# Layer A's small matmuls in groups of 32 columns

## The chip, the cores and the metric

One core of a Trainium2 chip. The core has a matrix engine (TensorE; its weight loads are shown apart as PEld), VectorE (DVE), ScalarE (ACT), GpSimd (POOL) and SyncE (SP), and 16 DMA engines that move data between the chip's memory and the on-chip buffers. Each engine works through its own queue of instructions in order; semaphores tell one engine that another has finished. The metric is the time of one execution on the device, in microseconds (us): the median of several runs.

## The reference

Four layers, A B A B, over x of 2048 rows by 640. Only layer A matters here: a transformer with a recurrent memory, 32 heads of 192, segments of 32 rows behind 8 memory rows.

```
for s in range(n_seg):                       # 64 segments
    xs = x[:, s*seg_len:(s+1)*seg_len, :]
    h = concatenate([mem, xs], axis=1)       # 8 + 32 rows
    q, k, v = h @ Wq, h @ Wk, h @ Wv         # per head
    scores = (q @ k^T) * scale
    scores = where(mask, scores, -1e9)
    o = softmax(scores) @ v
    o = o @ Wo
    mem = o[:, :M, :]                        # the next segment's memory
    outs.append(o[:, M:, :])
```

The memory ties the segments together: no projection of a segment can be finished before the output of the segment before it is known.

## The kernel before, in words

Each layer A has a preparation (`A_pre`), which computes what does not depend on the memory (keys, queries and values of the last 8 rows of all segments), and the chain (`A_chain`), which runs over the 64 segments one after the other. Layer A runs twice, so there are 128 segments. The order of the chain's instructions on each engine is the order in which the program writes them (`manual_schedule`).

A segment works on its 32 heads in four rounds of eight heads each; even segments run the rounds 0 to 3, odd ones 3 to 0, so that the weights of the turning round stay in place. The rows of `hT` are 8 memory rows and the first 24 of the segment; the last 8 rows come from the preparation's results, loaded as `kqb` and `vb` by GpSimd's DMA queue. Scores are held as 80 keys by 4 times 80 queries: 64 for a pair of heads' 32 rows and 16 for their last 8.

One round is made of these steps:
- Projections (`project`, L988): Q, K and V, each 5 pieces of 128 inputs, each piece 4 matmuls of 32 weight columns (`hT`) by 384 moving columns. The four go to partitions 0, 32, 64 and 96 of the result (`tile_position=(0, 32 * g)`), so that they use the array's four groups of 32 columns. Q and K are copied by ScalarE to `raw` (L998, one buffer) and transposed by VectorE into `QT` (L1006 to L1008) and `KT` (L1003); GpSimd adds the last 8 rows' parts (L964 to L967). V is copied into `Vp` by ScalarE (L1017) and VectorE (L1019).
- `scores`: a mask matmul (L1025, 80 weight columns) and six score matmuls (L1030, 80 weight columns by 80 or 160) into `ps_s`. `weigh` lets ScalarE take the exponential (L1085) into `E`.
- `sums` (L1099): a matmul of ones by `E`, 80 weight columns by 320, back into `ps_s`; ScalarE takes Ln and Exp of it (L1104, L1105) and VectorE multiplies `E` (L1106).
- `attend` (L1038): for each of two halves four matmuls of 128 weight columns (`Vp`) by 80. One 128-row part of the output holds two heads, so that it takes two of the four matmuls, added up. ScalarE and VectorE copy the result to `OT` (L1044, L1045) and the last rows' share to `otb` (L1051 to L1054), which GpSimd's queue stores.
- `wo_round` (L1067): 12 steps of 4 matmuls, 32 weight columns by 160, added up in `ps_w` over all rounds.

The rounds overlap. In round n the TensorE stream is: Q projection of n+1, `attend` of n-1, scores of n, K projection of n+1, `sums` of n, in round 1 also the output round of round 0, V projection of n+1. The first projections of a segment are Q, K and V of round 0 and Q and K of round 1. The segment ends with the last V projection (the second round's output matmuls between its pieces), the last scores, the third `attend`, `sums`, the third output round, the last `attend`, and the last output round. Then VectorE transposes the memory rows out of `ps_w` (L1220, L1221) into the next `hT`.

`keep_busy` (L1074) issues matmuls whose result nobody reads, at the segment's end, before waits; `fill` (L1080) issues weight loads of a single column that nobody uses: 2 in each segment (`SEG_FILL`), and 86 or 79 in a layer's first segment (`FILL`).

Weights: part of them stays in the buffer; 3 of 5 pieces of Q, K and V share slots between two rounds. `load_slot` reloads a slot on SyncE's queue as soon as round 0's projection has read it, and `load_wo` reloads the shared output weights after the first output round (`wo_rows`). SyncE's loads of a segment are 18: Q 3, K 6, V 3, output 6.

Of the kernel before, what the change touches and what calls it, by code (L numbers as in the profile page):

```python
# [17 lines left out]
SLOTS = {"Q": 3, "K": 3, "V": 3}  # L18
LN_EPS = 1e-5

FILL = {0: 86, 2: 79}
SEG_FILL = 2

LATE = 64512
ARENA = 202752
# [2 lines left out]
def ap3(ap, dims):  # L28
    return bass.AP(tensor=ap.tensor, offset=ap.offset, ap=[list(d) for d in dims])
# [86 lines left out]
class Kernel:  # L116
# [799 lines left out]
    def A_chain(self, xn_dram, at_dram, li, load_slot, piece, load_wo, late_wo, wo_mid, wo_end, low):  # L916
        nc, tc, KC, NSEG = self.nc, self.tc, self.KC, self.NSEG
        scale = float(self.Dh) ** -0.5
        NR = 4
        with tc.tile_pool(name=f"A{li}_ch", reuse_waits="tile", bufs=1) as sp, \  # L920
# [3 lines left out]
            KT = sp.tile([P, 6, 80], BF16, name="KT")  # L924
            QT = sp.tile([P, 2, 4, 80], BF16, name="QT")
            Vs = [sp.tile([P, 896], BF16, name=f"Vp{i}") for i in range(2)]
# [11 lines left out]
            def load_rows(s):  # L938
                nc.gpsimd.dma_start(out=xr[8:32, :], in_=xn_dram[32 * s:32 * s + 24, :])
# [61 lines left out]
            def to_rows(raw, m):  # L1001
                if m == "K":
                    nc.vector.transpose(out=KT[:, :, 0:64], in_=raw[:, :].rearrange("p (c j) -> p c j", j=64))  # L1003
                else:
                    rv = raw[:, :].rearrange("p (x i j) -> p x i j", i=3, j=64)
                    nc.vector.transpose(out=QT[:, :, 0:4:3, 0:64], in_=rv[:, :, 0:3:2, :])  # L1006
                    nc.vector.transpose(out=QT[0:64, :, 1, 0:64], in_=rv[0:64, :, 1, :])
                    nc.vector.transpose(out=QT[64:P, :, 2, 0:64], in_=rv[64:P, :, 1, :])  # L1008

            def v_rows(pv, n, which="ax"):  # L1010
                for x in range(2):
# [6 lines left out]
                    else:  # L1018
                        nc.vector.tensor_copy(out=o, in_=i)  # L1019

            def scores():

                S = pop.tile([P, 512], F32, name="ps_s", tag="s", bufs=2)
                m = self.mk[0:80, :]
                nc.tensor.matmul(S[0:80, 0:320], lhsT=self.ident[0:80, 0:80], rhs=ap3(m, [list(m.ap[0]), [0, 4], [1, 80]]),  # L1025
                                 start=True, stop=False, skip_group_check=True)
                for x in range(2):
                    for i, q0, q1 in ((0, 0, 1), (1, 1, 3), (2, 3, 4)):
                        c0 = 160 * x + (80 if i == 2 else 0)
                        nc.tensor.matmul(S[0:80, c0:c0 + 80 * (q1 - q0)], lhsT=KT[:, 3 * x + i, :], rhs=QT[:, x, q0:q1, :],  # L1030
                                         start=False, stop=(x == 1 and i == 2), skip_group_check=True)
                return S

            def attend(E, n, OT=None):
                O = [pop.tile([P, 512], F32, name=f"ps_o{x}", tag=f"o{x}") for x in range(2)]
                for x in range(2):
                    for k, e, i in ((0, 0, 0), (320, 1, 2), (128, 0, 1), (192, 1, 1)):
                        nc.tensor.matmul(O[x][:, 80 * i:80 * i + 80], lhsT=Vs[n % 2][0:80, 448 * x + k:448 * x + k + 128],  # L1038
                                         rhs=E[0:80, 160 * x + 80 * e:160 * x + 80 * e + 80], start=(k == 0),
                                         stop=(k == 192), skip_group_check=True)  # L1040
                if OT is None:
                    OT = sp.tile([P, 6, 64], BF16, name="OT", tag="OT")
                o = [x[:, 0:240].rearrange("p (i q) -> p i q", q=80) for x in O]
                nc.scalar.activation(out=OT[:, 0:3, :], in_=o[0][:, :, 0:64], func=ACT.Copy)  # L1044
                nc.vector.tensor_copy(out=OT[:, 3:6, :], in_=o[1][:, :, 0:64])  # L1045
                return OT, o
# [15 lines left out]
            def wo_round(W, r, OT, first, last, part=range(12)):  # L1062
                w = low[:, 0:7680] if last_wo == r else wo_end[:, :] if r in (0, 3) else wo_mid[:, 7680 * (r - 1):7680 * r]
                for i in part:
                    c, q = i % 6, 32 * (i // 6)
                    for g in range(4):
                        nc.tensor.matmul(W[32 * g:32 * g + 32, 0:160], lhsT=OT[:, c, q:q + 32],  # L1067
                                         rhs=w[:, 640 * i + 160 * g:640 * i + 160 * g + 160], start=(first and i == 0),
                                         stop=(last and i == 11), tile_position=(0, 32 * g), skip_group_check=True)

            def keep_busy(ps, n, w=384):

                for _ in range(n):
                    nc.tensor.matmul(ps[:, 0:w], lhsT=self.ident[:, :], rhs=wo_mid[:, 0:w], start=True, stop=True,  # L1074
                                     skip_group_check=True)

            def fill(n):

                for _ in range(n):
                    nc.tensor.ldweights(self.ident[:, 0:1])  # L1080

            def weigh(last):
                S = scores()
                E = sp.tile([P, 384], BF16, name="E3", tag="raw") if last else sp.tile([P, 320], BF16, name="E", tag="E")
                nc.scalar.activation(out=E[0:80, 0:320], in_=S[0:80, 0:320], func=ACT.Exp, scale=scale)  # L1085
                return S, E
# [9 lines left out]
                        kqs.append(load_kqb(*turns[at + 2]))  # L1096

            def sums(S, E):
                nc.tensor.matmul(S[0:80, 0:320], lhsT=ap3(self.ones_blk[0:80, :], [list(self.ones_blk[0:80, :].ap[0]), [0, 80]]), rhs=E[0:80, 0:320], start=True, stop=True,  # L1099
                                 skip_group_check=True)  # L1100

            def normalise(S, E):
                rc = S[0:80, 0:320]
# [17 lines left out]
            for s in range(NSEG):  # L1121
# [6 lines left out]
                def q_or_k(m, n):  # L1128
                    ps = pqp.tile([P, 512], F32, name="ps_qk", tag="qk")
                    project(hT, ps, m, n, s, range(KC))  # L1130
                    return to_raw(ps, "OT" if m == "K" and n == 0 else "raw")
# [11 lines left out]
                if s == 0:  # L1143
                    fill(FILL[li])
                to_rows(q_or_k("K", 0), "K")
# [10 lines left out]
                for n in range(L):  # L1156
                    raw = q_or_k("Q", n + 1)
                    if n > 0:
                        OT, o = attend(Ep, n - 1)
                        tails_after(n - 1)  # L1160
                    S, E = weigh(False)
                    to_rows(raw, "Q")
                    if n > 0:
                        otb = keep_tail(o)
                    next_kq(s, n)
                    if n > 0:
                        store_tail(otb, s, order[n - 1])
                    to_rows(q_or_k("K", n + 1), "K")
                    sums(S, E)
                    normalise(S, E)  # L1170
                    if n == 1:
                        wo_round(W, order[n - 1], OT, True, False)
                        if n == 1:
                            if s < NSEG - 1:
                                load_wo(order[L])
                            else:
                                tails = [self.fetch_tails(tb, low) for tb in range(2)]
                    if n + 1 < L:
                        pv = v_banks()
                        project(hT, pv, "V", n + 1, s, range(KC))  # L1180
                        v_rows(pv, n + 1)
                    Ep = E
# [5 lines left out]
                v_rows(pv, L)  # L1188
                S, E = weigh(True)
                OT, o = attend(Ep, L - 1, KT[:, :, 0:64])  # L1190
                tails_after(L - 1)
                otb = keep_tail(o, True)
                next_kq(s, L)
                store_tail(otb, s, order[L - 1])
                wo_round(W, order[L - 2], OT1, False, False, range(6, 8))
                sums(S, E)
                wo_round(W, order[L - 2], OT1, False, False, range(8, 12))
                normalise(S, E)
# [2 lines left out]
                    hx_transpose(hT, range(1))  # L1201
                wo_round(W, order[L - 1], OT, False, False)
                idle = pqp.tile([P, 512], F32, name="ps_idle", tag="qk")
                keep_busy(idle, 4, 96)
                OT, o = attend(E, L)
                tails_after(L)
                if s == NSEG - 1:
                    self.first_tails = tails, [self.spread_tails(0, tails[0], low, "vvss")]
                if s + 1 < NSEG:
                    hx_transpose(hT, range(1, 4))  # L1210
                    if s + 2 < NSEG:
                        load_rows(s + 2)
                keep_busy(idle, 5, 230)
                wo_round(W, order[L], OT, False, True)
                keep_busy(idle, 5, 230)
                fill(SEG_FILL)
                if s + 1 < NSEG:
                    wt = sp.tile([P, KC, 32], F32, name="wt", tag="raw")
# [86 lines left out]
```

## Time and profile before

| what | value |
|---|---|
| runs | 3599.22 us median of 3 (3597.11 to 3600.25) |
| the profiled execution: its span | 3590.5 us |
| granted TensorE clock, mean | 0.993 |
| instructions in the span | 168460 |
| DMA | 929.38 MB, mean 259 GB/s |
| one projection quad to the next, 4 x 384 columns | 162 ns |
| one output quad to the next, 4 x 160 columns | 69 ns |
| one `attend` matmul to the next, 128 x 80 | 35 to 36 ns |

The span is that of one execution under the profiler, from its first to its last instruction; a run's time has the launch around it, which makes the 3599.22 us of the median 8.7 us more than the span. In an answer on groups of instructions a line shows the kernel's line, the engine, the operation, what it writes and reads, how often, its busy time, and the idle time of the engine before it with what ended that. In a timeline the first two columns are start and duration in us. Matmuls overlap: their ends are modelled, and a better measure of a stream is the distance from one start to the next.

### The profile page before, as it was taken

How to read it: one execution, taken by the hardware profiler on the slowest of the kernel's cores; microseconds unless marked ns; L12 is line 12 of the kernel's file. 1: busy time of each engine (PE TensorE's matmuls, PEld its weight loads, DVE VectorE, ACT ScalarE, POOL GpSimd, SP SyncE). 2: the span in 40 equal slices, each digit the busy share in tenths (PEclk: the TensorE clock that was granted, in tenths of full speed). 3: DMA queues.
4: the chain of work that ended last, by engine and by line, in shares of the span. 5: the costliest groups of instructions: out<-in, count | busy, mean ns of one | idle time of the engine just before them, and what ended most of it. 6: DMA issues, size and time to landing. Idle time of an engine off the chain costs nothing.

```text
span 3590.5 us, 168460 instructions
## 1 busy us (share of the span) xinstructions
PE 3465.5 (97%) x70978; PEld 2268.6 (63%) x71399; DVE 2327.0 (65%) x6320; ACT 2032.0 (57%) x5233; POOL 1589.1 (44%) x4173
## 2 busy tenths in 40 slices
PE   9989999999999999999999899999999999999999
PEld 7756666666666666655377566666666666666553
DVE  5466666667666666746633566666666666676465
ACT  3356666666566656646432556666666666666463
POOL 3445555555555555530123455555545555555400
PEclk9999999999999999999999999999999999999999
DMA  8988888888788878860476878887888888888600
GB/s 311 334 290 288 281 295 282 278 292 299 278 284 295 289 277 278 295 224 3 146 272 217 290 275 287 290 291 278 285 294 279 290 282 292 292 281 287 222 1 30
DMA packets 452689, 929.38 MB, mean 259 GB/s; under 512 B 75338, under 2 KB 218330, under 8 KB 448858
## 3 DMA queue, kind: packets, MB, share of 16 engines
q1 hardware_dynamic: 382266, 817.56, 64.0%
q0 software_dynamic: 67744, 87.80, 7.9%
q8 instruction: 557, 9.13, 1.0%
q10 hardware_dynamic: 1920, 13.24, 0.9%
q14 instruction: 202, 1.65, 0.1%
HBM read 848.50 MB, written 73.73 MB: 257 GB/s over the span
## 4 chain that ended last, share of the span: by engine, by line
PE 55%; DMA 20%; issue 9%; DVE 7%; POOL 5%; ACT 4%; SPq 1%; PEld 0%; POOLq 0%; ACTq 0%; DVEq 0%
PE ps_qk L988 17%; DMA arena<-wo_rows 7%; DMA Vp<-vb 6%; PE ps_v L988 6%; PE ps_w L1067 6%; PE ps_pre L878 3%; PE ps_o L1038 3%; PE ps_s L1030 3%; DVE hT L943 2%; PE ps_s L1099 2%; DMA arena<-in_A_Wv_dram 2%; PE ps_s L1025 2%; PE ps_pre L902 2%; PE ps_idle L1074 2%; PE kv L1260 1%
## 5 line engine op out<-in xcount | busy, mean ns | idle before, releaser
L988 PEld LDWEIGHTS <-hT 128*32 128x32 bf16 x30720 | 746.5, 96 | 431.9 <-DVE hT L1221 27.2
L988 PE MATMUL ps_qk<-arena,hT 128*32 128x384 bf16 x20480 | 998.8, 328 | 14.6 <-DMA arena<-in_A_Wq_dram 4.2
L998 ACT ACTIVATE raw<-ps_qk 128x384 bf16<-128x384 f32 x1024 | 502.0, 490 | 383.7 <-PE ps_s L1099 250.9
L988 PE MATMUL ps_v<-arena,hT 128*32 128x384 bf16 x10240 | 534.6, 328 | 8.7 <-DMA arena<-in_A_Wv_dram 8.4
L971 POOL DMA_DIRECT2D Vp<-vb x512 | 258.4, 505 | 611.4 <-PE ps_o L1038 465.6
L1067 PE MATMUL ps_w<-arena,OT 128*32 128x160 bf16 x18432 | 446.1, 234 | 11.4 <-DMA arena<-wo_rows 10.4
L1003 DVE STREAM_TRANSPOSE KT<-raw 128x384 bf16<-128x384 bf16 x512 | 296.0, 578 | 194.5 <-ACT raw L998 190.5
L1067 PEld LDWEIGHTS <-OT 128*32 128x32 bf16 x18432 | 322.7, 96 | 103.8 <-ACT OT L1044 22.3
L1006 DVE STREAM_TRANSPOSE QT<-raw 128x256 bf16<-128x256 bf16 x512 | 227.9, 445 | 237.5 <-ACT raw L998 195.5
L959 POOL DMA_DIRECT2D kqb<-kqb x512 | 290.9, 568 | 168.9 <-POOL KT L967 147.3
L1019 DVE CAST Vp<-ps_v 64x384 bf16<-64x384 f32 x512 | 286.2, 559 | 113.6 <-ACT Vp L1017 90.0
L1106 DVE TENSOR_TENSOR E<-E,ps_s 80x320 bf16<-80x320 bf16 x512 | 247.4, 483 | 142.7 <-ACT ps_s L1105 142.3
L1058 POOL DMA_DIRECT2D otb<-otb x512 | 282.7, 552 | 128.1 <-DVE otb L1054 100.0
L1017 ACT ACTIVATE Vp<-ps_v 64x384 bf16<-64x384 f32 x512 | 246.1, 481 | 138.4 <-PE ps_v L988 122.9
L1038 PEld LDWEIGHTS <-Vp 80*128 80x128 bf16 x4096 | 189.9, 99 | 123.1 <-issue 80.5
L1038 PE MATMUL ps_o<-E,Vp 80*128 80x80 bf16 x4096 | 233.0, 201 | 31.8 <-DMA Vp<-vb 15.0
L1085 ACT ACTIVATE E<-ps_s 80x320 bf16<-80x320 f32 x512 | 221.4, 432 | 68.0 <-PE ps_s L1030 33.6
L951 ACT ACTIVATE Vp<-ps_w 32x160 bf16<-32x160 f32 x512 | 150.3, 294 | 155.1 <-DVE wt L1220 138.4
L964 POOL COPY QT<-kqb 128x64 bf16<-128x64 bf16 x512 | 124.5, 243 | 254.8 <-PE ps_s L1030 248.5
L1030 PE MATMUL ps_s<-QT,KT 128*80 128x80 bf16 (+1 forms) x3072 | 233.2, 213 | 1.6 <-POOL KT L967 1.5
L1104 ACT ACTIVATE ps_s<-ps_s 80x320 f32<-80x320 f32 x512 | 214.7, 419 | 31.2 <-PE ps_s L1099 31.2
L1030 PEld LDWEIGHTS <-KT 128*80 128x80 bf16 x3072 | 205.4, 119 | 28.7 <-issue 18.3
(156 smaller groups left out, 5446.4 us busy)
## 6 DMA issues: line engine op xcount, KB each, us to landing
arena<-wo_rows SPq DMA_DIRECT2D x780, 320.0 KB, 6.8
arena<-in_A_Wq_dram SPq DMA_DIRECT2D x427, 384.0 KB, 4.4
arena<-in_A_Wv_dram SPq DMA_DIRECT2D x427, 384.0 KB, 6.6
arena<-in_A_Wk_dram SPq DMA_DIRECT2D x768, 192.0 KB, 4.6
kqb<-kqb POOLq DMA_DIRECT2D x512, 48.0 KB, 5.1
arena<-in_A_Wk_dram SPq DMA_DIRECT2D x43, 384.0 KB, 7.8
vb<-arena POOLq DMA_DIRECT2D x128, 112.0 KB, 6.3
Vp<-vb POOLq DMA_DIRECT2D x512, 28.0 KB, 4.8
```

The source lines that it names most:

```text
L959: nc.gpsimd.dma_start(out=kqb[:], in_=self.kqb_d[r, :, s, :])
L971: nc.gpsimd.dma_start(out=Vs[n % 2][64:80, :], in_=self.vb_d[s, r].rearrange("g t f -> (g t) f"))
L988: nc.tensor.matmul(o[32 * g:32 * g + 32, 0:384], lhsT=hT[:, b, :], rhs=rhs, start=(i == 0), stop=(i == KC - 1), tile_position=(0, 32 * g), ...
L998: nc.scalar.activation(out=raw[:], in_=ps[:, 0:384], func=ACT.Copy)
L1003: nc.vector.transpose(out=KT[:, :, 0:64], in_=raw[:, :].rearrange("p (c j) -> p c j", j=64))
L1017: nc.scalar.activation(out=o, in_=i, func=ACT.Copy)
L1019: nc.vector.tensor_copy(out=o, in_=i)
L1030: nc.tensor.matmul(S[0:80, c0:c0 + 80 * (q1 - q0)], lhsT=KT[:, 3 * x + i, :], rhs=QT[:, x, q0:q1, :], start=False, stop=(x == 1 and i == 2 ...
L1038: nc.tensor.matmul(O[x][:, 80 * i:80 * i + 80], lhsT=Vs[n % 2][0:80, 448 * x + k:448 * x + k + 128], rhs=E[0:80, 160 * x + 80 * e:160 * x ...
L1058: nc.gpsimd.dma_start(out=self.otb_d[:, s, 96 * r:96 * r + 96], in_=otb[:, :, :].rearrange("p c t -> p (c t)"))
L1067: nc.tensor.matmul(W[32 * g:32 * g + 32, 0:160], lhsT=OT[:, c, q:q + 32], rhs=w[:, 640 * i + 160 * g:640 * i + 160 * g + 160], start=(firs ...
L1106: nc.vector.tensor_tensor(out=E[0:80, 0:320], in0=E[0:80, 0:320], in1=rc, op=ALU.mult)
```

## The change

Mask, scores, sums, attention and the filler matmuls are split along their weight columns into matmuls of at most 32 columns, each with a `tile_position` of its own, as the projections and the output round already are. 80 keys become three groups (32, 32, 16). In `attend` each group of 32 output rows belongs to one head, so the part that holds two heads no longer needs two added matmuls: 8 matmuls become 24. Per `scores` 7 matmuls become 21, per `sums` 1 becomes 3. The filler calls get other counts and widths, and each filler becomes four matmuls. Each matmul has its own weight load. The constants of `fill` change too.

```diff
-FILL = {0: 86, 2: 79}
-SEG_FILL = 2
+FILL = {0: 25, 2: 78}
+SEG_FILL = 0
...
+            keys = ((0, 32), (32, 64), (64, 80))
+
             def scores():
...
-                nc.tensor.matmul(S[0:80, 0:320], lhsT=self.ident[0:80, 0:80], rhs=ap3(m, [list(m.ap[0]), [0, 4], [1, 80]]),
-                                 start=True, stop=False, skip_group_check=True)
+                for k0, k1 in keys:
+                    nc.tensor.matmul(S[k0:k1, 0:320], lhsT=self.ident[0:80, k0:k1], rhs=ap3(m, [list(m.ap[0]), [0, 4], [1, 80]]),
+                                     start=True, stop=False, tile_position=(0, k0), skip_group_check=True)
                 for x in range(2):
                     for i, q0, q1 in ((0, 0, 1), (1, 1, 3), (2, 3, 4)):
                         c0 = 160 * x + (80 if i == 2 else 0)
-                        nc.tensor.matmul(S[0:80, c0:c0 + 80 * (q1 - q0)], lhsT=KT[:, 3 * x + i, :], rhs=QT[:, x, q0:q1, :],
-                                         start=False, stop=(x == 1 and i == 2), skip_group_check=True)
+                        for k0, k1 in keys:
+                            nc.tensor.matmul(S[k0:k1, c0:c0 + 80 * (q1 - q0)], lhsT=KT[:, 3 * x + i, k0:k1],
+                                             rhs=QT[:, x, q0:q1, :], start=False, stop=(x == 1 and i == 2),
+                                             tile_position=(0, k0), skip_group_check=True)
...
             def attend(E, n, OT=None):
...
-                    for k, e, i in ((0, 0, 0), (320, 1, 2), (128, 0, 1), (192, 1, 1)):
-                        nc.tensor.matmul(O[x][:, 80 * i:80 * i + 80], lhsT=Vs[n % 2][0:80, 448 * x + k:448 * x + k + 128],
-                                         rhs=E[0:80, 160 * x + 80 * e:160 * x + 80 * e + 80], start=(k == 0),
-                                         stop=(k == 192), skip_group_check=True)
+                    for i in range(3):
+                        for g in range(4):
+                            e = (4 * i + g) // 6
+                            v = 448 * x + 128 * i + 32 * g + 64 * e
+                            nc.tensor.matmul(O[x][32 * g:32 * g + 32, 80 * i:80 * i + 80], lhsT=Vs[n % 2][0:80, v:v + 32],
+                                             rhs=E[0:80, 160 * x + 80 * e:160 * x + 80 * e + 80], start=(i == 0),
+                                             stop=(i == 2), tile_position=(0, 32 * g), skip_group_check=True)
...
             def keep_busy(ps, n, w=384):
...
-                    nc.tensor.matmul(ps[:, 0:w], lhsT=self.ident[:, :], rhs=wo_mid[:, 0:w], start=True, stop=True,
-                                     skip_group_check=True)
+                    for g in range(4):
+                        nc.tensor.matmul(ps[32 * g:32 * g + 32, 0:w], lhsT=self.ident[:, 0:32], rhs=wo_mid[:, 0:w], start=True,
+                                         stop=True, tile_position=(0, 32 * g), skip_group_check=True)
...
             def sums(S, E):
-                nc.tensor.matmul(S[0:80, 0:320], lhsT=ap3(self.ones_blk[0:80, :], [list(self.ones_blk[0:80, :].ap[0]), [0, 80]]), rhs=E[0:80, 0:320], start=True, stop=True,
-                                 skip_group_check=True)
+                ones = self.ones_blk[0:80, :]
+                for k0, k1 in keys:
+                    nc.tensor.matmul(S[k0:k1, 0:320], lhsT=ap3(ones, [list(ones.ap[0]), [0, k1 - k0]]), rhs=E[0:80, 0:320],
+                                     start=True, stop=True, tile_position=(0, k0), skip_group_check=True)
...
-                keep_busy(idle, 4, 96)
+                keep_busy(idle, 1, 256)
                 OT, o = attend(E, L)
...
-                keep_busy(idle, 5, 230)
+                keep_busy(idle, 1, 384)
                 wo_round(W, order[L], OT, False, True)
-                keep_busy(idle, 5, 230)
+                keep_busy(idle, 2, 512)
                 fill(SEG_FILL)
```

## The prediction

> **What bounds the kernel now.** I read the page first, then segments of the two layer A chains: 2 x 64 of them, some 2,690 us of the 3,590.5 us span. From the first projection of a segment (called S) to the next, the trace has 21.14 us in the mean of 124 inner segments (shortest 20.56). TensorE is busy 97% by modelled ends, so its starts matter, and what ends its waits.
>
> ```profile
> PE 3465.5 (97%) x70978; PEld 2268.6 (63%) x71399; DVE 2327.0 (65%) x6320; ACT 2032.0 (57%) x5233; POOL 1589.1 (44%) x4173
> ...
> q8 instruction: 557, 9.13, 1.0%
> ```
>
> Of the page: TensorE runs 142,377 matmuls and weight loads, and the queue for instructions moves 557 packets, 16 KB each. The built program has 142,652 TensorE instructions, 557 times 256: this queue brings TensorE's own code, one packet for every 256 instructions.
>
> The waits of TensorE, longest first:
>
> ```profile
> PE ps_w L1067 <- issue: 16.4, 36, 1.2
> PE ps_o L1038 <- DMA Vp<-vb: 15.0, 39, 1.0
> PE ps_w L1067 <- DMA arena<-wo_rows: 10.4, 23, 1.0
> PE ps_v L988 <- DMA arena<-in_A_Wv_dram: 8.4, 9, 3.2
> ```
>
> The first is a wait for nothing that the profile shows; the others are loads that come late. One segment in order of time, weight loads of TensorE:
>
> ```profile
> 1003.78 0.11 PEld L1099 LDWEIGHTS <-ones_blk 80*80 80x80 bf16 x1
> 1004.04 0.26 PEld L1067 LDWEIGHTS <-OT 128*32 128x32 bf16 x16
> 1004.26 0.17 PEld L1067 LDWEIGHTS <-KT 128*32 128x32 bf16 x5
> 1005.04 0.74 PEld L1067 LDWEIGHTS <-KT 128*32 128x32 bf16 x43 [0.61 <-issue]
> ```
>
> The output round of 48 stops after 5 and goes on 0.61 us later. In the chains such stops (over 0.2 us, no semaphore awaited) stand at one place, instruction 194 or 195 modulo 256, 51 of 55; a segment passes that place four times. Over all 557 packets the next such place is never passed earlier than 1.24 us after the packet's end: the packet asked for on entering one block of 256 brings the next. So **a block cannot start before the fetch asked for at the start of the block before it has landed.** The four block starts, medians of 123 segments from the instruction packets and matmul starts:
> - block entered at S+0.50: packet 0.65 us later, 1.04 us long; next block entered 6.04 us after
> - S+6.55: 1.88 later, 0.95 long; next 4.88 after
> - S+11.43: 3.07 later, 1.02 long; next 5.54 after
> - S+16.97: 1.12 later, 1.11 long; next 4.47 after
>
> With 1.35 us from the packet's end to use (1.24 at least, 1.55 the median at the third), a fetch takes 3.0, 4.2, 5.4 and 3.6 us. The third already ties with its block. The reason for the spread is in the same segment's windows:
>
> ```profile
> 1008.66:1010.16 1.50, 1.50 (x40) 0.99 (x44) 0.38 (x3) 1.26 (x5) 0.77 (x2) 1.00 0.20 46
> 1010.16:1013.46 3.30, 3.30 (x75) 1.94 (x67) 2.65 (x7) 2.30 (x5) 1.12 (x5) 1.00 0.87 266
> 1013.46:1025.90 12.44, 12.19 (x298) 7.83 (x290) 8.81 (x24) 8.77 (x24) 6.69 (x20) 1.00 1.03 375
> 1025.90:1029.70 3.80, 3.59 (x117) 2.96 (x123) 2.84 (x9) 0.74 (x3) 2.42 (x6) 1.00 0.37 116
> ```
>
> The last three columns are the granted clock, the DMA share and GB/s. S is 1008.66: from S+4.8 to S+17.2 the DMA engines are full (1.03, 375 GB/s) with the 5.51 MB of weights of a segment, and an instruction packet queues among them.
>
> **The change part by part.** *Switches removed.* Between 32-column streams (projection: a quad of 384 columns every 162 ns) and full-width matmuls the next start is 95 to 100 ns later than the stream needs, 127 ns after the sums. I count 20 such switches a segment, 2.0 us. After the change none is left inside a segment. *Work.* Mask, scores and sums keep their columns; groups start 3 to 4 ns apart. Attention: 8 matmuls 36 ns apart (0.28 us) become 6 quads of 80 columns at 36 ns (0.22), by the output round's quads (160 columns, 69 ns). No row shows 80-column quads; by instruction rate (86 instructions in 0.75 us after the stop above, 115 per us) the 48 take 0.42. I take 0.22, since queued instructions start 3 to 4 ns apart; the other end costs 4 x 0.2 = 0.8 us a segment.
>
> *What of the 2.3 us is exposed.* Round 0: nothing. Scores wait for the transposed K (S+3.66), and attention for its softmax, 3.2 us after the last score (VectorE transposes, ScalarE copy, Ln, Exp, VectorE multiply), so it stays at S+7.13. Round 1 is TensorE's own: second attention at S+11.2 instead of 11.7, its third output round and projections with it. Round 2 hangs on the 3.2 us again; last attention S+17.4 instead of 18.0 at best. Then the last output round waits for its weights: the last weight packet ends at S+19.30 in the mean, the last matmul runs 0.63 us later at the earliest, the next S follows 0.90 us after (memory rows through VectorE). So without fetches the period is 20.83, 0.31 less. The loads start with round 0, which does not move, so their end does not either.
>
> *Idle filler* (`keep_busy`, 14 matmuls, 1.16 us) becomes 4 quads (0.69 us); it lies before waits for the evicted OT and hT: nothing. The first segment's fill of 86 and 79 weight loads (12 ns each) becomes 25 and 78: under 1 us. SyncE and GpSimd issue the same DMAs.
>
> *Code added.* 260 weight loads and matmuls a segment, less fill and separate waits: 1,024 becomes 1,280 in the built program, five blocks instead of four. By the same count modulo 256 they begin at the value projection of round 0 (S+1.8), inside the first attention (S+7.15), at the fourth Q projection, in the last value projection and at the last attention. Left alone, TensorE reaches the last three at S+10.37, 3.4 us later, and 3.6 us later. Against the rows:
> - Entered at 7.15, a fetch as of S+6.55 (4.2, taken as 4.3): 11.45, a stop of 1.1 us.
> - Entered at 11.45, as of S+11.43 (5.4): 16.85, where TensorE stands since 14.85: 2.0 us.
> - Entered at 16.85, as of S+16.97 (3.6): 20.45. Mask and scores take 0.6 us to 17.45, then Exp (0.8 to the sums) and softmax (1.8) let the last attention begin at 20.05: 0.4 us.
> - From the last attention 0.82 to the last output round (0.875 now), 0.78 for it, 0.90 to the next S: 22.95.
>
> That is the low end, 1.8 us over 21.14. These rows profit from TensorE's sequencer running ahead, about 60 instructions, before a block is entered. After a stop it has not: the next packet then began 1.1 us after the restart near S+17, so with the 2.8 us that the loaded row adds (4.36 us after instruction B-61, where unloaded preparation stages show 1.6), the three are 5.4, about 5.3 to 6.2, and 3.8: stops of 2.1, 1.9 to 2.8 and 0.5, period 24.05 to 24.8. That is the high end. I take 23.8, nearer to it since the first entry stands behind attention's wait and the others behind stops: 2.66 x 126 = 335 us. Against the profiled execution 3590.5 + 335 = 3925; the median of the runs lies 8.7 us above its span, so 3935.
>
> The Trainium skill speaks against these stops: "Runtime: NRT & Kernel Launch", section Instruction fetch mechanics, has blocks of 16 KiB fetched while the current one runs, and a crossing mostly hidden. The block size agrees with the trace; that it is hidden does not hold at the third row above (slack 1.55 us against a floor of 1.24). By that rule the time would be that of the first rival.
>
> **The rivals.** *Fetches keep up, faster.* If code were asked for more than a block ahead, only weights would bind: 0.31 x 126 = 39 us, 3560; 3510 if loads end 0.4 us sooner as output weights are asked for earlier. For it: other waits hide some of each stop. Against: the floor of 1.24 us, which half of the segments come within 0.3 us of at the third block. It decides from a fetch under 3.2 us in the full stretch. Chance 0.12.
>
> *Fetches keep up, but issue does not, no change.* Attention at 0.42 us gives back up to 0.8 us, more than the 0.31: about 3600. Against: 3 to 4 ns starts in every quad. Chance 0.03.
>
> *Fetches bind and the clock falls too.* At 1319.0 TensorE idled 1.54 us, and from 1322.04 the granted clock was 0.5 for 3.41 us. Stops of 2 us in each segment would bring such windows; at half clock the 2 us of matmuls after the third stop take 2 us more, of which some 1.2 lie under the softmax chain: 0.8 to 1.5 us on 23.8, so 4035 to 4125. Against: 1.91 us of idling at 1764.8 brought none. Chance 0.15. In the Trainium skill "TensorE: Matmul & The Clock Gate", section What you observe and its table, an idle window sets half rate; which idling would do it here no run shows.
>
> **How the numbers follow.** Forecast 0.70, the rivals 0.12, 0.03, 0.15. 3935 is the forecast's; its own range is 3720 to 4050, wider below than 22.95 (3825) for fetches that start earlier when the stops thin out the queue. To leave out no more than 2 in 10 I go from 3700 to 4110, into the third rival. A measurement of this kernel tells 0.2% from no change: slower by more 0.85, within 0.03, faster 0.12.
>
> **What would show it.** Right: 685 or so packets on the instruction queue; "issue" waits of TensorE far over 16.4 us, at attention, the fourth Q projection and the last value projection; segments near 23.8 us; DMA share of the chain below 0.82. The switches are seen right if the sums start within 10 ns of the stream's need. Wrong: segments under 21 us, stops still only a few tenths, or a second packet in flight before its block is entered.

## The result, and the profile after

| | time, us | span of the profiled execution, us | granted clock |
|---|---|---|---|
| before | 3599.73 (3597.11 to 3601.97, 4 runs) | 3590.5 | 0.993 |
| after | 3992.42 (3987.8 to 4005.25, 4 runs) | 3993.1 | 0.953 |

The change makes the kernel slower: the ratio is 1.11, with a 95% interval from 1.1065 to 1.1135. From one first projection to the next a segment takes 24.37 us in the mean of 124 inner segments (22.67 to 26.39) where it took 21.14. That is 3.23 x 126 = 407 us, as much as the whole difference of the spans (402.6 us).

From the page of the changed kernel: TensorE's busy time, the instruction queue, the DMA total, and the chain that ended last by engine.

```profile
PE 3295.8 (83%) x87584; PEld 2384.8 (60%) x87721; DVE 2328.2 (58%) x6320; ACT 2000.8 (50%) x5233; POOL 1589.5 (40%) x4173
...
DMA packets 452817, 931.48 MB, mean 233 GB/s; under 512 B 75338, under 2 KB 218330, under 8 KB 448858
...
q8 instruction: 685, 11.22, 1.1%
...
PE 46%; DVE 20%; issue 17%; ACT 11%; DMA 3%; PEld 2%; POOL 0%; ACTq 0%; SPq 0%; DVEq 0%; POOLq 0%
```

TensorE starts more instructions and is busy for 170 us less: the switches and the summed attention matmuls are gone, and the idle matmuls are shorter; how much each gives was not split. But 128 more packets of instructions came, one for each of the 2 x 64 segments, and "issue", a wait for nothing that the profile shows, is now 17% of the chain (9% before). Where it stands is in TensorE's waits, longest first (total us, times, longest us):

```profile
PE ps_v L988 <- issue: 318.8, 126, 4.2
PE ps_qk L988 <- issue: 128.3, 81, 2.9
PE ps_o L1046 <- DVE E L1117: 57.2, 128, 0.5
PE ps_qk L988 <- DVE hT L1232: 45.9, 125, 0.5
```

The longest total before was 16.4 us. The first line is one stop in every segment, inside the last V projection and in all 124 inner segments at the same place, after the fourth of its five pieces; the second comes in two of three segments, ahead of a Q projection. The timeline of one segment (start, duration, then engine, line and operation) shows both. S, the first projection, is at 1006.89:

```profile
1016.35 1.00 PE L988 MATMUL ps_v<-arena,hT 128*32 128x384 bf16 x19
1018.59 1.00 PE L988 MATMUL ps_qk<-arena,hT 128*32 128x384 bf16 x20 [1.24 <-issue]
...
1021.73 0.52 PE L988 MATMUL ps_v<-arena,hT 128*32 128x384 bf16 x7
1024.27 0.35 PE L988 MATMUL ps_v<-arena,hT 128*32 128x384 bf16 x4 [2.03 <-issue]
```

From S, the fourth Q projection stands at 11.7 us until its code is there. The last V projection stops between its fourth and its last piece and goes on at 17.4. The same segment in three windows (length, busy us of PE, PEld, DVE, ACT, POOL, then granted clock, DMA share, GB/s):

```profile
1006.89:1011.70 4.81, 4.81 (x128) 3.26 (x132) 3.08 (x11) 3.56 (x9) 1.91 (x6) 1.00 0.72 239
1011.70:1024.10 12.40, 8.85 (x310) 6.99 (x299) 7.61 (x19) 6.92 (x19) 5.76 (x16) 1.00 1.02 373
1024.10:1031.30 7.20, 6.48 (x224) 5.32 (x228) 4.32 (x15) 2.60 (x9) 3.49 (x9) 0.76 0.15 41
```

TensorE's idling lies in the middle window, where the DMA engines are full as before (1.02, 373 GB/s): 3.55 us of 12.40. The clock of 0.76 in the last window comes from a stretch at half rate (a granted clock of 0.5 for 3.41 us) that follows the stops.

The means over 124 segments, in us after S, put a place on the loss:

| start of | before | after | after less before |
|---|---|---|---|
| first attention | 7.12 | 7.05 | -0.07 |
| third V projection | 9.96 | 9.32 | -0.64 |
| fourth Q projection | 10.77 | 11.63 | +0.86 |
| second attention | 11.71 | 12.48 | +0.77 |
| last V projection | 13.72 | 13.91 | +0.19 |
| last scores | 15.08 | 18.11 | +3.03 |
| last attention | 18.46 | 21.65 | +3.19 |
| next S | 21.14 | 24.37 | +3.23 |

Grouping gains 0.64 us by the third V projection, loses 1.50 at the first stop, gains again, and loses 2.84 at the second.

### The profile page after: what moved, and what is told of

Read it like the earlier page. It is cut to its first block, busy times and chain, and to the rows that moved or that the text cites. A ratio compares the mean times of both kernels' runs of the same rounds, so it can differ in the third digit from the quotient of the medians.

```text
span 3993.1 us, 201134 instructions
## 1 busy us (share of the span) xinstructions
PE 3295.8 (83%) x87584; PEld 2384.8 (60%) x87721; DVE 2328.2 (58%) x6320; ACT 2000.8 (50%) x5233; POOL 1589.5 (40%) x4173
## 4 chain that ended last, share of the span: by engine, by line
PE 46%; DVE 20%; issue 17%; ACT 11%; DMA 3%; PEld 2%; POOL 0%; ACTq 0%; SPq 0%; DVEq 0%; POOLq 0%
PE ps_w L1075 9%; PE ps_qk L988 9%; PE ps_v L988 6%; PE ps_o L1046 4%; DVE hT L943 3%; ACT raw L998 3%; PE ps_pre L878 3%; DVE QT L1006 3%; ACT Vp L951 3%; PE ps_s L1034 2%; DVE E L1117 2%; DVE QT L1008 2%; ACT ps_s L1116 2%; PE kv L1271 2%; DVE KT L1003 2%
## 5 line engine op out<-in xcount | busy, mean ns | idle before, releaser
L988 PEld LDWEIGHTS <-hT 128*32 128x32 bf16 x30720 | 959.9, 97 | 884.6 <-issue 574.9
L988 PE MATMUL ps_v<-arena,hT 128*32 128x384 bf16 x10240 | 661.6, 329 | 327.2 <-issue 318.8
L1075 PE MATMUL ps_w<-arena,OT 128*32 128x160 bf16 x18432 | 554.7, 244 | 19.3 <-ACT OT L1052 12.1
L1075 PEld LDWEIGHTS <-OT 128*32 128x32 bf16 x18432 | 417.5, 100 | 69.0 <-ACT OT L1052 51.0
L1046 PE MATMUL ps_o<-E,Vp 80*32 80x80 bf16 x12288 | 252.9, 213 | 105.2 <-DVE E L1117 57.2
L1046 PEld LDWEIGHTS <-Vp 80*32 80x32 bf16 x12288 | 206.9, 104 | 179.0 <-issue 154.2
L1053 DVE CAST OT<-ps_o 128x192 bf16<-128x192 f32 x384 | 137.4, 358 | 291.0 <-PE ps_o L1046 285.8
L1034 PE MATMUL ps_s<-QT,KT 128*32 128x80 bf16 (+3 forms) x9216 | 244.4, 216 | 0.2
L1052 ACT ACTIVATE OT<-ps_o 128x192 bf16<-128x192 f32 x384 | 126.1, 328 | 223.7 <-PE ps_o L1046 208.0
L1034 PEld LDWEIGHTS <-KT 128*32 128x32 bf16 (+1 forms) x9216 | 195.2, 98 | 70.8 <-DVE KT L1003 45.9
```

Source lines behind the costliest of these rows:

```text
L988: nc.tensor.matmul(o[32 * g:32 * g + 32, 0:384], lhsT=hT[:, b, :], rhs=rhs, start=(i == 0), stop=(i == KC - 1), tile_position=(0, 32 * g), ...
L1034: nc.tensor.matmul(S[k0:k1, c0:c0 + 80 * (q1 - q0)], lhsT=KT[:, 3 * x + i, k0:k1], rhs=QT[:, x, q0:q1, :], start=False, stop=(x == 1 and i ...
L1046: nc.tensor.matmul(O[x][32 * g:32 * g + 32, 80 * i:80 * i + 80], lhsT=Vs[n % 2][0:80, v:v + 32], rhs=E[0:80, 160 * x + 80 * e:160 * x + 80 ...
```

## The experiments

The theory: the time is lost at the starts of blocks of 256 TensorE instructions whose fetch lands late while the DMA engines are full. Its rivals: the grouped matmuls cost the time themselves; or only the place of the block starts matters.

### The weights loaded once, after and before

```diff
+                if stay:
+                    return
...
-                        load_slot(m, order[NR - 1], b)
+                        load_slot(m, order[NR - 1], b, stay=True)
...
-                            if s < NSEG - 1:
-                                load_wo(order[L])
-                            else:
+                            if s == NSEG - 1:
```

> The changed kernel without the chain's reloads of Q, K, V and output weights (the slots keep what they hold, so the results are not the reference's); every TensorE instruction stays, 1280 a segment, but the DMA engines are nearly free. Theory fetch (a block of 256 TensorE instructions cannot start before its packet has landed, and packets queue among the weights): a fetch then takes about 3.4 us everywhere (1.1 to the packet, 0.95, 1.4), the block at the fourth Q projection stops 0.2 us at most and the others not: segments of 20.0 to 20.4 us against 21.14 of the kernel before, 3440 to 3510 us, and 30 to 80 us FASTER than the kernel before without its reloads. Theory narrow (the small matmuls of 32 columns themselves cost the time, in the array or in issue): 300 us or more SLOWER than the kernel before without reloads, 3800 us or more.

> The kernel before with the same reloads left out (results not the reference's). Only the other kernel's partner: segments lose the waits for late weights and the few stops at block starts. Both theories: 20.5 to 20.8 us a segment, 3510 to 3560 us.

Measured: the changed kernel 3394.41 us, ratio to the kernel before 0.9434 (0.9414 to 0.9454), segments of 19.65 us; the kernel before 3493.47 us, ratio 0.9713 (0.9692 to 0.9734), segments of 20.58. Of the changed kernel without reloads, the page and the waits of TensorE:

```profile
DMA packets 122736, 230.35 MB, mean 68 GB/s; under 512 B 38666, under 2 KB 83354, under 8 KB 118810
...
q8 instruction: 685, 11.22, 1.3%
```

```profile
PE ps_o L1048 <- DVE E L1119: 111.5, 376, 0.5
...
PE ps_o L1048 <- issue: 5.3, 2, 2.7
PE ps_v L990 <- issue: 5.1, 2, 2.6
```

The same 685 packets and the same matmuls, and the stops are gone: issue waits of the chain's tiles fall from 456 us in total to 12. The sign of the change turns, too: with free DMA engines grouping is worth 0.93 us a segment, with full ones it costs 3.23. Both kernels came out some 20 to 50 us below their ranges, and they are 99 us apart where 30 to 80 were expected. This shows that the loss hangs on the DMA load; it does not show yet that code is what comes late.

### All blocks half a block away

```diff
-FILL = {0: 25, 2: 78}
+FILL = {0: 153, 2: 206}
```

> The changed kernel with 128 more fill loads in a layer's first segment, so that each block of 256 starts half a block elsewhere. Theory fetch: every place in the stretch of full DMA engines is too dense, so the stops move and stay: 23.0 to 24.3 us a segment, 3840 to 3990 us. Theory place (only the chosen place of the blocks is unlucky): back under 3650 us. Theory narrow: the same 3990 within 0.5%.

Measured, in a single run: 4012.15 us, span 4010.4. In the first chain, half a block away, a segment takes 24.92 us, in the second, where the two shifts add up to a whole block, 24.04. The time is a little above the range of the fetch theory and far from the 3650 that the place alone would give. It is also within 0.5% of the changed kernel's 3992.42, as the narrow theory had it, so the time does not decide between fetch and narrow. The places of the stops do. TensorE's longest waits are:

```profile
PE ps_w L1075 <- issue: 177.3, 158, 3.8
PE ps_v L988 <- issue: 153.9, 63, 3.7
PE ps_s L1034 <- issue: 112.1, 62, 2.7
```

Taken apart by chain, the first has all the stops of the first and the third line and none in a V projection; the second has all those of the V projection, the place that they have in the changed kernel. The matmuls are the same, only the blocks begin elsewhere, and the stops went with them. The stretch of full DMA engines is 12 us long, and with five blocks in 24 us some starts fell into it in both places.

### Half of the change at a time

Attention alone in groups, and mask, scores and sums alone in groups, each 1152 instructions a segment, so 4.5 blocks. The edits are those parts of the change's diff; the idle matmuls stay as before.

> Only the attention is in column groups; mask, scores, sums and fillers as before: 1152 TensorE instructions a segment, 4.5 blocks, half of the added code. Fetch theory (each added block costs a stop while the DMA engines are full): after against before is +3.23 us a segment (24.37 against 21.14), and without the weight reloads the grouped form was 0.93 us a segment faster, so the fifth block costs 4.2 us; half of it is 2.1, less 0.4 us for the eight switches that go: segments near 22.8 us, time 3720 to 3870 us. Rival, that the groups of the scores and sums do the damage (three tiles of 32, 32 and 16 columns that share one accumulator bank): 3560 to 3620 us.

> Only mask, scores and sums are in column groups; the attention and its idle matmuls as before, two more one-column loads as filler: 1152 instructions a segment, 4.5 blocks. Fetch theory: 2.1 us of stops less 0.5 us of switches: segments near 22.7 us, time 3700 to 3860 us. Rival, that the damage is the attention's 24 matmuls in place of 8: 3530 to 3620 us.

Measured: attention alone 3836.83 us, ratio 1.065 (1.0623 to 1.0677), segments of 23.08 us; scores and sums alone 3823.14 us, ratio 1.0612 (1.058 to 1.0644), segments of 23.06; both lie inside the ranges of the fetch theory. Two different halves of the edit cost the same +1.94 and +1.92 us. Issue waits of the chain's tiles are 228 and 251 us, against 18 before and 456 after, so half of the added code brings half of the stops. Neither the attention's form nor that of the scores does the damage alone.

### Added code with nothing grouped

First, one more weight load ahead of every projection matmul, and 16 more one-column loads as filler, 1280 instructions:

```diff
+                        nc.tensor.ldweights(hT[:, b, :], tile_position=(0, 32 * g))
                         nc.tensor.matmul(o[32 * g:32 * g + 32, 0:384], lhsT=hT[:, b, :], rhs=rhs, start=(i == 0),
```

> The kernel before with each projection matmul's weights loaded twice (240 weight loads a segment, 32 columns each) and 16 more single-column fill loads: 1280 TensorE instructions a segment like the changed kernel, all matmuls as before. Theory fetch: stops at the block starts in the output round of round 0's block (1.4 us) and after it, segments of 22.7 to 23.6 us, 3790 to 3930 us. Theory narrow: the added loads lie under quads of 162 ns, so 3590 to 3640 us.

Measured 3986.51 us, ratio 1.1094 (1.106 to 1.1127), segments of 24.27 us: as slow as the change, and above the range. It is not the clean test that it looks like. Issue waits are 105 us only. The 20 matmuls of the first V projection take 1.22 us in place of 0.66, and the copy of the third Q projection begins 1.36 us after the start of its last matmul in place of 0.38. The doubled loads delay the results themselves.

Then in the waits of the segment's end, in place of 26 of the 28 idle instructions:

```diff
-                keep_busy(idle, 4, 96)
+                keep_busy(idle, 1, 96)
+                fill(40)
...
-                keep_busy(idle, 5, 230)
+                fill(50)
...
-                keep_busy(idle, 5, 230)
+                fill(64)
```

> The kernel before, no group added. The idle matmuls at the tail of a segment (waits of 0.44, 0.59 and 0.72 us) give way to one of them and 154 loads of one column, which at some 9 ns each fit into the same waits: 1152 instructions a segment, nothing added to the work. Fetch theory: half a block more, so up to 2.1 us of stops, less where the dense part of the code lies at the tail, where the DMA engines are free: segments 22 to 23.3 us, time 3700 to 3870 us. Rival, that the grouped matmuls themselves are slow and the count of instructions is nothing: 3580 to 3630 us.

Measured 3958.2 us, ratio 1.0987 (1.0959 to 1.1014), segments of 24.03 us, above the range. The clock fell as well when the idle matmuls went: 42 windows at half rate, 280 us together, against 9 and 55 us before. The added loads start 12 to 13 ns apart in the mean, not 9. Issue waits are 150 us. Inconclusive: several causes are mixed.

Then 128 loads, placed where the first of these three had shown no slower projection, once with and once without the reloads:

```diff
+LATE_ROUNDS = {(m, n) for m in "QKV" for n in range(1, 4)} - {("Q", 1)}
...
                         o = ps
+                        if (m, n) in LATE_ROUNDS and i > 0:
+                            nc.tensor.ldweights(hT[:, b, :], tile_position=(0, 32 * g))
```

> The kernel before with 128 weight loads of 32 columns more a segment, one ahead of each projection matmul in rounds 1 to 3 but the first of each group and the second Q projection: there doubled loads left the pace of a projection at 0.66 to 0.69 us for its 20 matmuls, where those of round 0 took 1.22. No group added, no work changed, idle matmuls kept: 1152 instructions a segment. Fetch theory: as the halves with groups (23.08 and 23.06 us a segment), without their gain of some 0.4 us: segments 22.8 to 23.8 us, time 3800 to 3930 us. Rival, that the grouped matmuls are what costs: 3600 to 3650 us.

> The kernel with 128 weight loads more, and the weights loaded once in place of in every segment (this leaves the rotating weights at those of the first load, so the result is not the reference's). Fetch theory: added code costs little where the DMA engines are free: within 40 us of the kernel before without reloads (3493 us), so 3480 to 3535 us. Rival, that the added loads or the blocks cost the same whatever the DMA engines do: the difference that the pair with reloads shows, 3700 us or more.

Measured: 3878.73 us with reloads, ratio 1.0784 (1.0735 to 1.0832), segments of 23.43 us; 3583.39 us without, ratio 0.9957 (0.994 to 0.9975), segments of 21.25. The first lies inside its range; the second is a miss, 90 us above its twin without the added loads. TensorE's waits, first with reloads, then without:

```profile
PE ps_w L1070 <- issue: 118.7, 116, 2.7
PE ps_o L1041 <- DVE E L1109: 47.4, 128, 0.4
PE ps_qk L991 <- issue: 45.3, 52, 2.3
PE ps_s L1033 <- issue: 30.8, 46, 2.4
```

```profile
PE ps_o L1043 <- DVE E L1111: 47.4, 128, 0.4
PE ps_v L411 <- ACT arena L424: 6.1, 6, 1.8
PE ps_pre L881 <- DVE next_xT L88: 3.7, 1, 3.7
PE ps_s L1035 <- issue: 3.7, 2, 2.7
```

The price without reloads, 21.25 - 20.58 = 0.67 us a segment, is hardly a fetch, since issue waits are only 7 us in all. The first attention waits for `E` in every segment (47.4 us, 128 times, in both runs). The copy of the second K projection begins 0.88 us after the start of the projection's last matmul in place of 0.59, and the first attention comes at S+7.42 in place of 7.13: that is 0.29 of the 0.67 us. The rest is lost by the third attention, at S+16.27 in place of 15.61; what loses it was not looked into. With reloads the price is 23.43 - 21.14 = 2.29. The part that hangs on the DMA load is 2.29 - 0.67 = 1.62 us, and the issue waits alone come close to it: 206 us against 18 in the kernel before are 1.49 us for each of 126 segments, and without reloads there are 7 us. Here nothing is grouped, and half a block of added code brings stops that come and go with the weights' traffic. With the halves above, three different edits of 1152 instructions have 206 to 251 us of such waits; the fourth, with the loads at the segment's end, has 150.

### Sums alone, paid for with filler

```diff
+            keys = ((0, 32), (32, 64), (64, 80))
...
+                for k0, k1 in keys:
+                    nc.tensor.matmul(S[k0:k1, 0:320], lhsT=ap3(ones, [list(ones.ap[0]), [0, k1 - k0]]), rhs=E[0:80, 0:320],
+                                     start=True, stop=True, tile_position=(0, k0), skip_group_check=True)
...
-                keep_busy(idle, 4, 96)
+                keep_busy(idle, 2, 192)
...
-                keep_busy(idle, 5, 230)
+                keep_busy(idle, 3, 384)
...
-                keep_busy(idle, 5, 230)
+                keep_busy(idle, 2, 512)
```

`SEG_FILL` becomes 0, and `FILL` 78 and 79, so that blocks begin where they did.

> Only the sums are in column groups (8 of the 20 switches go, 16 instructions more), paid for with the idle matmuls (14 become 7, wider) and the two loads: 1024 instructions a segment, blocks at the places of the kernel before. Fetch theory: no added stop, the switches' gain of up to 0.8 us a segment held back by the weights, whose last packet bounds a segment at 20.8 us: time 3540 to 3590 us, faster than both kernels. Rival, that groups of 32, 32 and 16 columns in one bank are slow in themselves: 3600 us or more.

Measured 3574.26 us, ratio 0.9931 (0.991 to 0.9951): faster than both kernels, by 0.7% against the one before, and inside the range. Segments take 20.95 us. Its longest waits of TensorE:

```profile
PE ps_o L1040 <- DVE E L1110: 45.5, 131, 1.7
PE ps_w L1069 <- issue: 32.9, 56, 1.8
PE ps_w L1069 <- DMA arena<-wo_rows: 18.6, 45, 1.1
```

Eight of the twenty switches are gone, and the gain of 0.19 us a segment is less than their some 0.1 us each: the first attention now waits for its softmax (S+7.13), the third output round for its code (median S+17.2), and the last one for its weights (S+20.1).

### Sums in two groups of unequal size

```diff
-            keys = ((0, 32), (32, 64), (64, 80))
+            keys = ((0, 64), (64, 80))
```

`SEG_FILL` is 8 and `FILL` 82 and 79 here.

> The sums in two column groups of 64 and 16 columns in place of 32, 32 and 16; eight more one-column loads keep 1024 instructions a segment and the blocks' places. If TensorE drains only between the full array and a part of it: as the three groups, 3574 us within 10 (20.9 us a segment). If it drains wherever the size of the tile changes (64 against 32 columns): the sums wait about 0.1 us on both sides again, 3590 to 3610 us.

Measured 3610.26 us, ratio 1.0037 (1.0019 to 1.0055), segments of 21.2 us, with 10 us of issue waits: at the upper end of what was expected if TensorE drains (runs empty) at a change of the tile's size. The idle matmuls are those of the run before, so they are not what made that one faster. The sums in three groups, then in two, and the projection that follows:

```profile
1000.16 0.31 PE L1103 MATMUL ps_s<-E,ones_blk 80*32 80x320 bf16 x3
1000.17 1.11 PE L988 MATMUL ps_v<-arena,hT 128*32 128x384 bf16 x20
```

```profile
1014.26 0.34 PEld L1103 LDWEIGHTS <-ones_blk 80*64 80x64 bf16 x2 [0.32 <-issue]
1014.26 0.56 PE L1103 MATMUL ps_s<-E,ones_blk 80*64 80x320 bf16 x2
1014.52 0.51 PE L988 MATMUL ps_v<-arena,hT 128*32 128x384 bf16 x7
```

Three groups of 32, 32 and 16 columns start within 10 ns, and the projection starts 10 ns after the first of them. With a group of 64, 0.25 us pass between the first and the second sums matmul: between a tile of 64 columns and one of 32 the next start comes later than the stream needs, on both sides of the larger one. The Trainium skill says this in "TensorEngine Tiling (Array Packing)", section Key Properties: a change of the tiling mode drains the engine, a change of the tile does not. The trace agrees and adds the price, about 0.1 us ahead of the 64 columns (projection to sums, 0.255 us for 384 columns that take 0.160) and 0.12 behind them (0.253 for 320 columns, 0.133).

## Why the prediction was right, and where its sizes were off

**What bounds.** The rule on block starts held over the new code: 685 packets, as forecast, and over all of them the next block's first matmul comes no earlier than 1.19 us after the packet's end. The weights no longer bind: their last packet ends at S+19.11 in the mean, the last output matmul runs at S+23.34. The DMA share of the chain fell from 0.82 to 0.72, as the forecast's sign had it (below 0.82). That the stops are made by fetches under load, and not by what the matmuls are, is shown by the runs with nothing grouped, by those without reloads, and by the stops that moved with the blocks.

**The places.** Block starts were forecast at S+1.8 and S+7.15, at the fourth Q projection, in the last V projection and at the last attention. Medians of 123 segments: S+1.80, 7.12, 11.81, 18.03 and 21.66, at those places.

**The stops.** The fetches took, from block start over packet to use, 2.21 + 1.05 + 1.38 = 4.64 us at S+7.12, 3.79 + 1.04 + 1.45 = 6.28 at S+11.81 and 1.13 + 1.05 + 1.42 = 3.60 at S+18.03. Forecast were 4.3 or 5.4, then 5.4 or up to 6.2, then 3.6 or 3.8. The dear one is the second: it cost a little more than the high end allowed. With the tail, 2.71 us from the last attention to the next S where 2.50 was forecast (0.82 + 0.78 + 0.90), the measured terms add up: 7.12 + 4.64 + 6.28 + 3.60 + 2.71 = 24.35.

One sign did not come as forecast: at attention TensorE has only 8.9 us of issue waits, 5 times. The last attention does begin with its block, 1.42 us after the packet's end, and 0.49 us after its softmax is ready (medians of 124), but the matmuls ahead of it run on into that time, and what idling there is stands under other names (`PE ps_o L1046 <- DVE hT L943`, 38.0 us). How much of the 0.49 us is the fetch, and how much the half clock of the output round before it, was not split.

**The sum.** The mis-sized step is the one that says "I take 23.8, nearer to it": 24.37 lies inside the high end of 24.05 to 24.8. (Added up from its own fetches, 7.15 + 5.4 + 5.3 to 6.2 + 3.8 + 2.5, that high end is 24.15 to 25.05; 24.37 lies in both.) The difference, 0.57 x 126 = 72 us, is that between the spans (3993.1 against 3925), and more than the 57 us between the times. That the forecast of the time came nearer than that of the segment is luck. It added the 8.7 us that the text ahead of it puts down to the launch, but a run is only 1.8 us longer than its own span (3994.92 and 3993.1); the rest of the 8.7 was that the profiled execution of the kernel before was quicker than the median of its runs.

**What grouping gains.** The 24 attention matmuls start within 0.20 and 0.19 us in the first two rounds, as taken (0.22, not 0.42), and within 0.31 and 0.30 in the last two (medians), where other streams' matmuls stand among them or the clock is halved. Round 0 does not move, as forecast: the first attention is at S+7.05 for 7.12. Without stops the gain is larger than the 0.31 us of the forecast, which the weights were to limit: 0.93 us where neither reloads nor stops bind, and the last attention at S+17.11 against 18.02 in that pair.

**Rivals.** Fetches that keep up, with or without issue that does: excluded by 24.37 us. The clock: it did fall, with 97 windows at half rate, 376 us together, against 9 and 55 us before. Segments in which such a window starts take 24.51 us (87), the others 24.03 (37), though their issue waits are no longer (3.55 and 3.64 us a segment). The 0.48 x 87 = 42 us are less than the 0.8 to 1.5 us a segment that the rival put on it, and by this comparison 0.34 of the 0.57 us a segment by which 23.8 was too low. The tail, too, is 2.55 us in the segments without a window and 2.79 in the others. The kernel would have been slow without it.

**Open.** It was not tried apart whether an instruction packet is late because it stands behind weight packets in the DMA engines or because memory is busy. Of the 4.72 us that reloads cost the changed kernel a segment, 3.5 stand as issue waits of TensorE; the half clock and what is queued behind the stops may take the rest, which was not split.

## What to carry to other kernels

Count an engine's instructions like bytes: set the time in which it runs 256 of them against the time from the request of the next 256 to their use, here 3 us where the DMA engines are little used and up to 6.3 us beside weight loads at 375 GB/s. In this kernel cutting the small matmuls into more pieces paid (0.93 us a segment) as long as no block ran out before the next one came, and cost 3.23 us where it did; so take first the cut that removes most waiting per added instruction, and pay for it with filler. A test that adds code must be run once without the load as well, since the added instructions have a price of their own.

## What the runs showed of the hardware that was not expected

*Groups run past each other.* With all matmuls in groups of 32 columns, a stream no longer ends before the next begins. In the changed kernel the 80 keys leave the fourth group idle, and a matmul of the next projection starts among the scores:

```profile
1010.45 0.35 PE L1034 MATMUL ps_s<-QT,KT 128*32 128x80 bf16 x12
1010.62 0.34 PE L988 MATMUL ps_qk<-arena,hT 128*32 128x384 bf16 x1
1010.64 0.27 PE L1034 MATMUL ps_s<-QT,KT 128*32 128x160 bf16 x6
1010.74 0.98 PE L988 MATMUL ps_qk<-arena,hT 128*32 128x384 bf16 x19
```

The projection's matmul at 1010.62 comes later in the program than the scores at 1010.64. That it is the one of the idle group is likely, but the trace does not name groups. The section of the Trainium skill named above has it that tiles work independently, and here the trace shows it. "Sums within 10 ns of the stream's need" was too modest: in rounds 0 to 2 the next stream starts 0.08 to 0.10 us ahead of the sums that stand before it in the program.

*Some results are handed over later.* Counted from the start of a projection's last matmul, ScalarE's copy of the second K projection begins 0.59 us later in the kernel before, 0.72 in the changed one and 0.88 where weight loads were added late, with reloads and without; that of the third Q projection 0.38, 0.50 and 1.10. That of the fourth Q projection is 0.38 both before and after the change. At the end of a segment the memory rows' transpose starts 0.33 us after the start of the last output matmul before the change and 0.48 after it. The runs show the delay, not its cause. Through the first attention it accounts for 0.29 of the 0.67 us a segment that the added loads cost without reloads; what it takes back of what the switches gave was not measured.
